# A scratch tile moved, dependences per 8 bytes, and new durations in the planner of a four-layer spectral kernel

## The chip, the cores and the metric

The kernel runs on one core of one Trainium2 chip. The metric is device time in microseconds (us), the median of several runs. The core has TensorE (PE; its weight loads are PEld), VectorE (DVE), ScalarE (ACT), GpSimd (POOL) and SyncE (SP, which here only issues DMAs). They run their own instruction streams and wait for each other by semaphores.

## The reference

x is 2048 rows of 448 bf16 values. Two kinds of layers alternate, each added to x:

```
x = x + A(layernorm(x));  x = x + B(layernorm(x))
x = x + A(layernorm(x));  x = x + B(layernorm(x))

A(x) = irfft2(rfft2(x) * (w_r + 1j * w_i))        # over rows and columns
B(x) = relu(x @ w1 + b1)**2 @ w2 + b2             # 448 -> 1792 -> 448
```

Both spectral layers (A) have the same weights, and so have both feed-forward layers (B).

## The kernel before

The 2048 rows lie as 16 tiles of 128 partitions (x_sb). A spectral layer is done by matmuls with constant matrices, in stages. Stage A (`stage_A`, matrices Fs or FA_sb) transforms inside a tile and leaves its result, by ScalarE, in the tile XA: each of the 16 tiles fills 8 of the 128 columns of every block of XA. Stage TD (TD_sb) transforms along d and reads all of XA; there are eight items p, taken in the order 1 to 7 and then 0, and ScalarE puts each result into U. Stage B (G_sb) transforms the long axis, from U into EF. Stage W multiplies by the weights: VectorE alone, in 12 tensor-tensor instructions of up to 904 elements a group, from EF over the scratch tile tmp into Z. Its groups are item 1 (on EF of item 1), items 2 and 3, 4 and 5, 6 and 7, and last item 0. In the first layer TensorE mirrors weights in between (J_sb), and w1_aux prepares w1 (ones). Stage Bi (H_sb) transforms back from Z into VT: eight matmuls for each item, in two PSUM tiles of four. Stage TI (TI_sb) is the inverse along d: ScalarE evicts it into TIo, which is an alias of the memory of XA. Stage AI (FI_sb) reads TIo and its result is added to x by VectorE (line 725). `ln_B` then prepares the layernorm of the feed-forward layer (a square on ScalarE, some short VectorE instructions, a root), and SP transposes the tile into yT by DMA.

In the feed-forward layer h_part (W1_sb, yT) fills hbuf and o_tile (W2_sb, hbuf) sums a tile of x. After an o_tile of the first feed-forward layer, `second_A` takes the layernorm for the next spectral layer: statistics, root, reciprocal, then two VectorE instructions that write y of the tile into yA, and stage A from there. yA holds eight tiles; it is an alias of the first half of tmp. U, EF, Z, hbuf and xb share one arena.

No instruction order is written by hand. Every instruction is first recorded (`_Sched.add`) with its engine, what it reads and writes, a cost and a latency. `_pages` cuts an access into pages, and a shared page makes a dependence: a read after a write, a write after a read or a write. Matmuls that share a PSUM tile form one unit. A unit's priority is the longest path behind it plus a bias set by hand for each stage and item. `schedule()` then takes, over all engines, the unit that can start first by the modelled times, with priority deciding between equals; a matmul unit is held back until all that the readers of its PSUM tile depend on, and that was recorded earlier, has been placed. The result is one fixed order for each engine. On the chip each instruction waits only for its recorded dependences, by semaphores, and behind those before it on its engine. The modelled times do not act on the chip themselves.

The lines that carry names in the trace: 455 is `mm`, 474 is `act`, 478 is `tt`, 482 is `cp`, 487 is `ts`. As these helpers record nearly every operation, groups are told apart by their tiles. What the memory aliases look like:

```python
        yA = tmp[:].rearrange("p a b c d -> p (a b c d)")[:, 0:8 * D].rearrange("p (t d) -> p t d", t=8)
        TIo = XA[:].rearrange("p a b c d -> p (a b c d)")[:, 0:NT * 2 * HD].rearrange("p (t g d) -> p t g d", t=NT, g=2)
        U = arena[:, 0:16 * 2 * LW].rearrange("p (c l) -> p c l", c=16)    # LW = 226, HD = 224, D = 448, NT = 16
```

Of the kernel before, what the change touches and what calls it, by code (L numbers as in the profile page):

```python
# [13 lines left out]
HD = 224  # L14
NT = 16
# [139 lines left out]
def _res(a):  # L155
    return a.ap() if isinstance(a, _PsAP) else a


def _pages(ap):

    if isinstance(ap, _PsAP):
        return [ap.tile]
    pat = list(ap.ap)
    row = pat[0][0]
    name = ap.tensor.name
    off = np.array([ap.offset % row if row else ap.offset])
    for step, cnt in pat[1:]:
        off = (off[:, None] + step * np.arange(cnt)[None, :]).reshape(-1)
    pg = np.unique(off * mybir.dt.size(ap.dtype) // 32)
    return [(name, int(i)) for i in pg]  # L170


class _Sched:
# [12 lines left out]
        self.reads_since = {}  # L186
        self.bias = 0.0

    def add(self, eng, fn, reads=(), writes=(), is_dma=False, cost=100.0, lat=150.0):
        op = _Op(eng, fn, is_dma, cost, lat)  # L190
        rk = [k for a in reads for k in _pages(a)]
        wk = [k for a in writes for k in _pages(a)]
        deps = {}
        for k in rk:
            w = self.last_write.get(k)
            if w is not None:
                deps[id(w)] = w
        for k in wk:
            w = self.last_write.get(k)
            if w is not None:  # L200
                deps[id(w)] = w
            for rd in self.reads_since.get(k, ()):
                deps[id(rd)] = rd
        for k in rk:
            self.reads_since.setdefault(k, []).append(op)
        for k in wk:
            self.last_write[k] = op
            self.reads_since[k] = []
        op.gdeps = [d for d in deps.values() if d is not op]
        op.deps = [d for d in deps.values() if d is not op and not (d.eng == "pe" and eng == "pe")]  # L210
        tile = writes[0].tile if eng == "pe" else None
        if tile is not None and tile.unit is not None:
            u = tile.unit
        else:
            u = _Unit(eng, tile)
            u.bias = self.bias
            u.seq = len(self.units)
            self.units.append(u)
            if tile is not None:
                tile.unit = u  # L220
        for a in reads:
            if isinstance(a, _PsAP):
                a.tile.readers.append(op)
        op.unit = u
        u.ops.append(op)
        return op

    def schedule(self):
# [25 lines left out]
        done = {}  # L254
# [10 lines left out]
        def ready_of(u):  # L265
            if u not in ready:
                r, off = 0.0, 0.0
                for op in u.ops:
                    for d in op.gdeps:
                        if d.unit is not u:  # L270
                            same = d.eng == u.eng and not d.is_dma
                            r = max(r, done[d] + d.lat - off)
                    off += op.cost
                ready[u] = r
            return ready[u]

        def pick_banks(n, now):
            best = None
            for b in range(0, NB, n):
                ok = [bank_user[i] is None or all(op in done for op in bank_user[i].readers) for i in range(b, b + n)]  # L280
                if all(ok):
                    f = max(bank_free[b:b + n])
                    key = (max(f, now), bank_free[b ^ 1] <= now and n == 1, f)
                    if best is None or key < best[0]:
                        best = (key, f, b)
            return best and best[1:]

        total = len(self.units)
        while total:
            choice = None  # L290
            for e in self.ENGINES:
                best = None
                avail = {}
                for u in cand[e]:
                    r = ready_of(u)
                    if u.tile is not None:
                        if u.tile.n not in avail:
                            avail[u.tile.n] = pick_banks(u.tile.n, free[e])
                        if avail[u.tile.n] is None:
                            continue  # L300
                        r = max(r, avail[u.tile.n][0])
                    start = max(r, free[e])
                    key = (start, -u.prio, u.seq)
                    if best is None or key < best[0]:
                        best = (key, u)
                if best is not None and (choice is None or best[0] < choice[0]):
                    choice = best
            assert choice is not None, "no unit can run"
            start, u = choice[0][0], choice[1]
            e = u.eng  # L310
            cand[e].remove(u)
            total -= 1
            if u.tile is not None:
                b = pick_banks(u.tile.n, start)[1]
# [8 lines left out]
            t = start  # L323
# [44 lines left out]
def _free(ap):  # L368
    n = 1
    for step, cnt in list(ap.ap)[1:]:  # L370
        n *= cnt
    return n


def bass_interleave_layers__spectral_gfnet__dense_activation_squared_relu__prompt_kernel(nc, A_x, A_w_r, A_w_i, B_x, B_w1, B_b1, B_w2, B_b2, out):
# [4 lines left out]
    sch = _Sched()  # L380

    with ExitStack() as es:
        onchip = set()

        def sb(name, shape, dt=BF16):
            t = es.enter_context(nc.sbuf_tensor(name, shape, dt))
            onchip.add(t.name)
            return t

        x_sb = sb("x_sb", [P, NT, 4 * P])  # L390
        XA = sb("XA", [P, 2, 2, 16, P])
# [6 lines left out]
        tmp = sb("tmp", [P, 8, 2, 2, LW])  # L398
        yA = tmp[:].rearrange("p a b c d -> p (a b c d)")[:, 0:8 * D].rearrange("p (t d) -> p t d", t=8)
        VT = sb("VT", [P, 2, 2, NT, 16, 8])  # L400
        xr = VT[:].rearrange("p a b t c j -> p (a b t c j)")[:, 0:NT * HD].rearrange("p (t d) -> p t d", t=NT)
        TIo = XA[:].rearrange("p a b c d -> p (a b c d)")[:, 0:NT * 2 * HD].rearrange("p (t g d) -> p t g d", t=NT, g=2)
        yT = sb("yT", [P, NT, 4, P])
        Wn = yT[:].rearrange("p a b c -> p (a b c)")[:, 0:2 * 16 * 225].rearrange("p (r k l) -> p r k l", r=2, k=16)
        Wt = sb("Wt", [P, 32, LW])
# [47 lines left out]

        def mm(o, lhsT, rhs, start, stop, skip=False):
            sch.add("pe", lambda e: e.matmul(_res(o), lhsT, rhs, start=start, stop=stop, skip_group_check=skip),  # L455
                    [lhsT, rhs], [o], cost=max(_free(rhs) / 2.4 + 6.0, 64.0), lat=200.0)

        def nfree(o, i):
            return _free(o) if not isinstance(o, _PsAP) else _free(i)

        def act(o, i, func=ACT.Copy, bias=None, scale=None):
            kw = {}
            rd = [i]
            c = (nfree(o, i) + 205.0) / 1.2
            if bias is not None:
                kw["bias"] = bias
                rd.append(bias)
                c += 60.0
            if scale is not None:
                kw["scale"] = scale  # L470
                if not isinstance(scale, float):
                    rd.append(scale)
                    c += 60.0
            sch.add("act", lambda e: e.activation(o, _res(i), func, **kw), rd, [o], cost=c)  # L474

        def tt(o, a, b, op, eng="dve"):
            rate = 0.96 if isinstance(a, _PsAP) or eng == "pool" else 1.92
            sch.add(eng, lambda e: e.tensor_tensor(o, _res(a), b, op), [a, b], [o], cost=_free(o) / rate + 65.0)  # L478

        def cp(o, i, eng="dve"):  # L480
            rate = 0.96 if isinstance(i, _PsAP) or eng == "pool" else 1.92
            sch.add(eng, lambda e: e.tensor_copy(o, _res(i)), [i], [o], cost=_free(o) / rate + 65.0)  # L482

        def ts(o, i, s1, s2, op0, op1=None, eng="dve"):
            rd = [i] + [s for s in (s1, s2) if s is not None and not isinstance(s, float)]
            kw = {} if op1 is None else {"op1": op1}
            sch.add(eng, lambda e: e.tensor_scalar(o, i, s1, s2, op0=op0, **kw), rd, [o],  # L487
                    cost=_free(o) * 0.83 + 265.0 if eng == "pool" else _free(o) / 1.92 + 65.0)

        def memset(o, v, eng="dve"):  # L490
            sch.add(eng, lambda e: e.memset(o, v), [], [o], cost=_free(o) / 1.92 + 60.0)

        def small(fn, reads, writes, cost=100.0):
            sch.add("dve", fn, reads, writes, cost=cost)


# [31 lines left out]
        def w1_aux():  # L528

            qs = []  # L530
            for i in range(4):
                f = slice(D * i, D * (i + 1))
                q = _Tile(1)
                qs.append((f, q))
                for blk in range(4):
                    mm(q[lambda b: ps[:, b, 0:D]], ones[:], W1_sb[:, blk, f], blk == 0, blk == 3)
                act(W1_sb[64:97, 3, f], q[lambda b: ps[64:97, b, 0:D]], ACT.Copy, scale=-1.0 / D)
                act(c_rem[64:97, f], q[lambda b: ps[64:97, b, 0:D]], ACT.Copy, scale=-1.0 / D)
            for r in (65, 67):
                dma("sp", W1_sb[r:r + 1, 3, :], B_b1.rearrange("(o f) -> o f", o=1))  # L540
            lo, c = W1_sb[96:97, 3, :], c_rem[96:97, :]
            tt(lo, c, lo, ALU.subtract)
# [369 lines left out]
```

## Time and profile before

| | |
|---|---|
| runs shown | 321.12 us median of 3 (320.16 to 321.24) |
| profiled execution | 323.18 us, of which the profile's span is 321.4 us |
| mean granted TensorE clock | 0.968 of 2.4 GHz |
| busy | PE 283.2 us (88%), DVE 195.9 (61%), ACT 184.4 (57%), POOL 17.1 (5%) |
| instructions | PE 1710 matmuls, DVE 606, ACT 381, POOL 34 |

Busy times are of the whole span. The kernel passes through a first spectral layer to about 70 us, a feed-forward layer to about 171 us, a second spectral layer to about 223 us and a second feed-forward layer. The busy share of an engine says little over all of them; the stage does. Matmuls overlap in their pipeline, so the distance of their starts is what TensorE needs for one, and the duration of a row of n like matmuls is n - 1 such distances and one whole duration. The same holds for evictions on ScalarE that follow each other.

### The profile page before, as it was taken

The page shows a single profiled execution, that of the slowest core. Times are in us where ns is not written, and L with a number is a line of the kernel's source. Part 1 is how long each engine was busy: PE and PEld are TensorE (multiplying, and loading weights), DVE is VectorE, ACT ScalarE, POOL GpSimd, SP SyncE. Part 2 cuts the span into 40 slices and gives each one's busy share as a digit, 9 for nine tenths or more (in the row PEclk, how much of TensorE's full clock was granted, in tenths as well). Part 3 has the DMA queues.
Part 4 walks back from the last instruction along what each step waited for, and adds up shares of the span by engine and source line. Part 5 has one row for each costly group of instructions (what it writes and reads, how often), then busy time and mean ns, then how long its engine had stood idle before and what let it go on. Part 6 is the DMA issues. An engine that isn't in the chain of part 4 may idle for free.

```text
span 321.4 us, 4833 instructions
## 1 busy us (share of the span) xinstructions
PE 283.2 (88%) x1710; PEld 168.5 (52%) x1710; DVE 195.9 (61%) x606; ACT 184.4 (57%) x381; POOL 17.1 (5%) x34
## 2 busy tenths in 40 slices
PE   0799895879999999999996966787999999999995
PEld 0466663748544544654454644464864454455442
DVE  5763998497684784576564489449733453474431
ACT  2479996899237437835713866479931741751720
POOL 3672000000000000000000000000000000000000
PEclk9989998999999999999999899599999999999999
DMA  7996000032100100030000000003701002005001
GB/s 231 423 382 175 1 2 1 0 77 56 35 1 0 24 10 1 2 65 2 0 0 2 0 0 2 2 0 65 101 14 46 0 22 70 0 14 107 4 14 43
DMA packets 25436, 16.04 MB, mean 50 GB/s; under 512 B 17666, under 2 KB 24322, under 8 KB 25412
## 3 DMA queue, kind: packets, MB, share of 16 engines
q1 hardware_dynamic: 25124, 15.44, 17.5%
q10 hardware_dynamic: 288, 0.30, 0.3%
q8 instruction: 13, 0.21, 0.3%
q14 instruction: 11, 0.09, 0.1%
HBM read 9.70 MB, written 1.84 MB: 36 GB/s over the span
## 4 chain that ended last, share of the span: by engine, by line
PE 73%; DVE 15%; ACT 6%; issue 3%; DMA 2%; POOL 1%; SPq 0%; DVEq 0%; ACTq 0%
PE ps L455 73%; DVE tmp L478 8%; DVE arena L478 3%; ACT arena L474 2%; ACT XA L474 2%; DVE x_sb L725 2%; DMA x_sb<-in_A_x_dram 1%; ACT VT L474 1%; DMA yT<-x_sb 1%; DVE st L567 1%; POOL Fs L487 1%; ACT sq_out L733 0%; DVE x_sb L773 0%; ACT W_sb L474 0%; DVE x_sb L482 0%
## 5 line engine op out<-in xcount | busy, mean ns | idle before, releaser
L474 ACT ACTIVATE arena<-ps 128x512 bf16<-128x512 f32 (+2 forms) x172 | 98.6, 590 | 56.9 <-PE ps L455 54.6
L455 PE MATMUL ps<-yT,W_sb 128*128 128x512 bf16 (+1 forms) x560 | 98.3, 336 | 2.0 <-ACT XA L474 1.3
L455 PE MATMUL ps<-W_sb,arena 128*128 128x448 bf16 x448 | 86.9, 352 | 0.0
L455 PEld LDWEIGHTS ps<-yT,W_sb 128*128 128x128 bf16 x560 | 54.7, 98 | 44.5 <-issue 2.8
L478 DVE TENSOR_TENSOR arena<-arena 128x512 bf16<-128x512 bf16 (+1 forms) x140 | 51.5, 372 | 40.1 <-ACT arena L474 34.9
L455 PEld LDWEIGHTS ps<-W_sb,arena 128*128 128x128 bf16 x448 | 43.8, 98 | 39.3
L474 ACT ACTIVATE XA<-ps 128x512 bf16<-128x512 f32 (+2 forms) x50 | 32.8, 679 | 20.2 <-PE ps L455 20.0
L773 DVE SCALAR_TENSOR_TENSOR x_sb<-ps,r,arena 128x448 bf16<-128x448 f32 x32 | 21.9, 684 | 31.3 <-PE ps L455 31.3
L455 PE MATMUL ps<-H_sb,arena 128*128 128x256 bf16 x128 | 22.2, 330 | 10.2 <-DVE arena L478 8.9
L725 DVE SCALAR_TENSOR_TENSOR x_sb<-ps,x_sb 128x448 bf16<-128x448 f32 x32 | 18.9, 620 | 16.4 <-PE ps L455 16.4
L474 ACT ACTIVATE VT<-ps 128x512 bf16<-128x512 f32 (+1 forms) x36 | 18.5, 552 | 10.9 <-PE ps L455 10.6
L455 PEld LDWEIGHTS ps<-H_sb,arena 128*128 128x128 bf16 x128 | 13.8, 116 | 18.4 <-DVE arena L478 12.8
L474 ACT ACTIVATE mv<-mv,epst 128x1 f32<-128x1 f32 (+1 forms) x24 | 7.1, 294 | 28.3 <-DVE mv L568 27.8
L567 DVE BATCH_NORM_STATS2 st<-x_sb 128x6 f32<-128x448 bf16 x32 | 19.4, 616 | 3.1 <-DMA x_sb<-in_A_x_dram 2.6
L733 ACT ACTIVATE sq_out<-x_sb 128x448 bf16<-128x448 bf16 x32 | 18.1, 568 | 3.0 <-DVE x_sb L725 2.8
L455 PE MATMUL ps<-Fs,x_sb 128*128 128x256 bf16 x32 | 10.2, 335 | 10.8 <-POOL Fs L487 8.9
L478 DVE TENSOR_TENSOR tmp<-arena 128x904 bf16<-128x904 bf16 (+1 forms) x16 | 8.9, 567 | 15.6 <-ACT arena L474 15.5
L455 PE MATMUL ps<-arena,G_sb 128*128 128x452 bf16 (+1 forms) x72 | 14.6, 335 | 3.9 <-ACT arena L474 3.9
L455 PE MATMUL ps<-XA,FI_sb 128*128 128x448 bf16 (+1 forms) x72 | 14.8, 332 | 3.2 <-ACT XA L474 2.3
L455 PE MATMUL ps<-TD_sb,XA 128*128 128x226 bf16 x128 | 16.0, 278 | 1.1 <-ACT XA L474 0.8
L478 DVE TENSOR_TENSOR tmp<-tmp,Wt 128x904 bf16<-128x904 bf16 (+1 forms) x32 | 16.4, 564 | 0.1
L455 PE MATMUL ps<-TI_sb,VT 128*128 128x224 bf16 x128 | 14.4, 259 | 1.5 <-ACT VT L474 1.5
(51 smaller groups left out, 202.9 us busy)
## 6 DMA issues: line engine op xcount, KB each, us to landing
out_dram<-x_sb SPq DMA_DIRECT2D x16, 112.0 KB, 1.7
W_sb<-in_B_w_dram SPq DMA_DIRECT2D x1, 1568.0 KB, 17.2
x_sb<-in_A_x_dram SPq DMA_DIRECT2D x3, 448.0 KB, 6.3
W_sb<-in_B_w_dram SPq DMA_DIRECT2D x1, 1344.0 KB, 15.5
yT<-in_A_w_r_dram SPq DMA_DIRECT2D x1, 900.0 KB, 8.9
yT<-in_A_w_i_dram SPq DMA_DIRECT2D x1, 900.0 KB, 10.4
H_sb<-c_H SPq DMA_DIRECT2D x1, 896.0 KB, 11.4
G_sb<-c_G SPq DMA_DIRECT2D x1, 672.0 KB, 8.1
```

The source lines that it names most:

```text
L455: sch.add("pe", lambda e: e.matmul(_res(o), lhsT, rhs, start=start, stop=stop, skip_group_check=skip), [lhsT, rhs], [o], cost=max(_free(rh ...
L474: sch.add("act", lambda e: e.activation(o, _res(i), func, **kw), rd, [o], cost=c)
L478: sch.add(eng, lambda e: e.tensor_tensor(o, _res(a), b, op), [a, b], [o], cost=_free(o) / rate + 65.0)
L487: sch.add(eng, lambda e: e.tensor_scalar(o, i, s1, s2, op0=op0, **kw), rd, [o], cost=_free(o) * 0.83 + 265.0 if eng == "pool" else _free(o ...
L567: small(lambda e, t=t: e.bn_stats(st[:, t, 0:6], x_sb[:, t, 0:D]), [x_sb[:, t, 0:D]], [st[:, t, 0:6]], 540.0)
L725: small(lambda e, xx=xx, r=r, i=i: e.scalar_tensor_tensor(out=xx, in0=_res(r), scalar=1.0, in1=xx, op0=ALU.mult, op1=ALU.add, accum_out=sd ...
L733: sch.add("act", lambda e, i=i: e.activation(sq_out[:, i % 2, :], x_sb[:, i, 0:D], ACT.Square, accum_out=sd[:, i, 1:2]), [x_sb[:, i, 0:D]] ...
L773: small(lambda e: e.scalar_tensor_tensor(out=o, in0=_res(i), scalar=r2[:, t, 0:1], in1=xb[:, t, :], op0=ALU.mult, op1=ALU.add), [i, r2[:, ...
```

## The change

The diff has three parts. TIo becomes an alias of tmp, the scratch of stage W, and no longer of XA. Pages are of 8 bytes in place of 32. And the costs and latencies that the planner is given change: a matmul costs N / 2.4 + 2.5 ns (at least 56) and not + 6 (at least 64); an ACT instruction from PSUM (N + 61) / 1.2, one from SBUF (N + 112) / 1.2, and not (N + 205) / 1.2 for both, with 93 ns and not 60 for a bias or a scale operand; VectorE instructions get 4 ns more; the short ones 75 ns and not 100; the default latency is 130 ns and not 150; and a matmul unit that depends on another unit may start 80 ns later.

```diff
@@ _pages
-    pg = np.unique(off * mybir.dt.size(ap.dtype) // 32)
+    pg = np.unique(off * mybir.dt.size(ap.dtype) // 8)
@@ _Sched.add
-    def add(self, eng, fn, reads=(), writes=(), is_dma=False, cost=100.0, lat=150.0):
+    def add(self, eng, fn, reads=(), writes=(), is_dma=False, cost=100.0, lat=130.0):
@@ _Sched.schedule, ready_of
-                            r = max(r, done[d] + d.lat - off)
+                            r = max(r, done[d] + d.lat + (80.0 if u.eng == "pe" else 0.0) - off)
@@ the kernel's tiles
-        TIo = XA[:].rearrange("p a b c d -> p (a b c d)")[:, 0:NT * 2 * HD].rearrange("p (t g d) -> p t g d", t=NT, g=2)
+        TIo = tmp[:].rearrange("p a b c d -> p (a b c d)")[:, 0:NT * 2 * HD].rearrange("p (t g d) -> p t g d", t=NT, g=2)
@@ mm
-                    [lhsT, rhs], [o], cost=max(_free(rhs) / 2.4 + 6.0, 64.0), lat=200.0)
+                    [lhsT, rhs], [o], cost=max(_free(rhs) / 2.4 + 2.5, 56.0), lat=195.0)
@@ act
-            c = (nfree(o, i) + 205.0) / 1.2
+            c = (nfree(o, i) + (61.0 if isinstance(i, _PsAP) else 112.0)) / 1.2
             if bias is not None:
-                c += 60.0
+                c += 93.0
             if scale is not None:
                 if not isinstance(scale, float):
-                    c += 60.0
+                    c += 93.0
@@ tt (cp alike)
-            sch.add(eng, lambda e: e.tensor_tensor(o, _res(a), b, op), [a, b], [o], cost=_free(o) / rate + 65.0)
+            sch.add(eng, lambda e: e.tensor_tensor(o, _res(a), b, op), [a, b], [o], cost=_free(o) / rate + 69.0)
@@ ts
-                    cost=_free(o) * 0.83 + 265.0 if eng == "pool" else _free(o) / 1.92 + 65.0)
+                    cost=_free(o) * 0.83 + 245.0 if eng == "pool" else _free(o) / 1.92 + 69.0)
@@ small
-        def small(fn, reads, writes, cost=100.0):
+        def small(fn, reads, writes, cost=75.0):
```

## Rows read from the trace of the kernel before

**Rows 1.** The page's chain that ended last: share of the span by engine.

```profile
PE 73%; DVE 15%; ACT 6%; issue 3%; DMA 2%; POOL 1%; SPq 0%; DVEq 0%; ACTq 0%
```

**Rows 2.** Busy time by stretch, us from the start; PEclk: granted clock.

```profile
core 0: us, PE busy (x) PEld busy (x) DVE busy (x) ACT busy (x) POOL busy (x), PEclk, DMA share, GB/s
...
48.00:52.50 4.50, 0.33 (x2) 0.10 (x1) 4.50 (x12) 2.79 (x7) 0.00 (x0) 1.00 0.00 2
52.50:58.20 5.70, 4.89 (x28) 3.32 (x28) 2.27 (x2) 4.30 (x9) 0.00 (x0) 0.70 0.00 0
58.20:69.67 11.47, 9.08 (x71) 6.49 (x72) 8.59 (x42) 10.11 (x25) 0.00 (x0) 1.00 0.14 29
...
133.00:171.30 38.30, 38.29 (x214) 20.91 (x215) 23.57 (x70) 18.07 (x39) 0.00 (x0) 1.00 0.07 15
...
204.10:211.50 7.40, 6.08 (x28) 3.60 (x28) 0.26 (x1) 4.35 (x9) 0.00 (x0) 0.59 0.01 2
```

**Rows 3.** TensorE in time, 24 to 60 us: start, duration, group, idle before.

```profile
32.95 0.60 PE L455 MATMUL ps<-H_sb,arena 128*128 128x256 bf16 x4
...
52.51 4.80 PE L455 MATMUL ps<-H_sb,arena 128*128 128x256 bf16 x27 [0.63 <-DVE arena L478]
...
58.25 1.61 PE L455 MATMUL ps<-TI_sb,VT 128*128 128x224 bf16 x15 [0.85 <-ACT VT L474]
```

**Rows 4.** VectorE in time, 24 to 60 us.

```profile
31.41 0.96 DVE L478 TENSOR_TENSOR arena<-tmp 128x226 bf16<-128x226 bf16 x4
32.74 1.29 DVE L478 TENSOR_TENSOR tmp<-arena 128x904 bf16<-128x904 bf16 x2 [0.37 <-ACT arena L474]
...
50.84 1.91 DVE L478 TENSOR_TENSOR arena<-tmp 128x452 bf16<-128x452 bf16 x6
```

**Rows 5.** TensorE in time, 174 to 226 us.

```profile
175.33 4.10 PE L455 MATMUL ps<-TD_sb,XA 128*128 128x226 bf16 x24 [0.78 <-ACT XA L474]
179.22 1.79 PE L455 MATMUL ps<-arena,G_sb 128*128 128x452 bf16 x8
...
184.48 0.72 PE L455 MATMUL ps<-H_sb,arena 128*128 128x256 bf16 x4
...
204.12 1.68 PE L455 MATMUL ps<-H_sb,arena 128*128 128x256 bf16 x7 [0.52 <-DVE arena L478]
206.48 4.13 PE L455 MATMUL ps<-H_sb,arena 128*128 128x256 bf16 x20 [0.69 <-ACT VT L474]
```

**Rows 6.** VectorE in time, 174 to 214 us.

```profile
183.68 0.97 DVE L478 TENSOR_TENSOR arena<-tmp 128x226 bf16<-128x226 bf16 x4
185.74 1.29 DVE L478 TENSOR_TENSOR tmp<-arena 128x904 bf16<-128x904 bf16 x2 [1.09 <-ACT arena L474]
...
202.46 1.91 DVE L478 TENSOR_TENSOR arena<-tmp 128x452 bf16<-128x452 bf16 x6
```

**Rows 7.** ScalarE in time, 174 to 187 us.

```profile
179.47 2.56 ACT L474 ACTIVATE arena<-ps 128x904 bf16<-128x904 f32 x3 [0.58 <-PE ps L455]
182.26 3.37 ACT L474 ACTIVATE arena<-ps 128x904 bf16<-128x904 f32 x4 [0.24 <-PE ps L455]
```

**Rows 8.** TensorE in time, 128 to 136 us.

```profile
130.72 0.93 PE L455 MATMUL ps<-XA,FI_sb 128*128 128x448 bf16 x4 [0.25 <-ACT XA L474]
131.48 1.04 PE L455 MATMUL ps<-FA_sb,tmp 128*128 128x256 bf16 x8
133.01 1.91 PE L455 MATMUL ps<-FA_sb,tmp 128*128 128x256 bf16 x16 [0.49 <-DVE sd L478]
```

**Rows 9.** ScalarE in time, 39 to 48 us.

```profile
40.08 2.07 ACT L474 ACTIVATE VT<-ps 128x512 bf16<-128x512 f32 x4
```

**Rows 10.** All engines in time, 0 to 25 us.

```profile
12.40 0.60 ACT L474 ACTIVATE XA<-ps 128x512 bf16<-128x512 f32 x1 [0.39 <-PE ps L455]
...
12.90 0.29 ACT L474 ACTIVATE mv<-mv,epst 128x2 f32<-128x2 f32 x1
...
14.13 0.27 PE L455 MATMUL ps<-Fs,x_sb 128*128 128x256 bf16 x1 [1.76 <-issue]
```

**Rows 11.** All engines in time, 24 to 72 us.

```profile
69.67 2.56 PE L455 MATMUL ps<-yT,W_sb 128*128 128x256 bf16 x22 [1.27 <-ACT XA L474]
```

More of the change, by code (lines that the diff above doesn't have):

```diff
@@ L477, in tt @@
             rate = 0.96 if isinstance(a, _PsAP) or eng == "pool" else 1.92
-            sch.add(eng, lambda e: e.tensor_tensor(o, _res(a), b, op), [a, b], [o], cost=_free(o) / rate + 65.0)
+            sch.add(eng, lambda e: e.tensor_tensor(o, _res(a), b, op), [a, b], [o], cost=_free(o) / rate + 69.0)
         def cp(o, i, eng="dve"):
             rate = 0.96 if isinstance(i, _PsAP) or eng == "pool" else 1.92
-            sch.add(eng, lambda e: e.tensor_copy(o, _res(i)), [i], [o], cost=_free(o) / rate + 65.0)
+            sch.add(eng, lambda e: e.tensor_copy(o, _res(i)), [i], [o], cost=_free(o) / rate + 69.0)
         def ts(o, i, s1, s2, op0, op1=None, eng="dve"):
```

## The prediction

> **What bounds the kernel now.** I began with the chain that ended last [rows 1]: TensorE carries 73% of it and VectorE 15%, so most of the span is matmuls in a row, and only what leaves TensorE idle can be won. The table of stretches [rows 2] says where that is. From 133 to 171.3 us TensorE is busy 38.29 of 38.30 us, and a planner cannot shorten that. In 48 to 52.5 us it is busy 0.33 of 4.50 us while VectorE is busy for all 4.50 us: that is the W product. Behind it, in 52.5 to 58.2 us, the granted clock is 0.70, a mixture of the two levels, 1.2 and 2.4 GHz; in the second layer's like stretch, 204.1 to 211.5 us, it is 0.59. So each spectral layer has a stage where VectorE sets the end, and a tail where TensorE works off what waited for VectorE, mostly at 1.2 GHz. Then comes a stage (58.2 to 69.67 us) where ScalarE is busy 10.11 of 11.47 us and TensorE only 9.08.
>
> I then read TensorE's and VectorE's order of time in both spectral layers [rows 3 to 6]. After W, 27 inverse matmuls (H_sb) start at 52.51 us and take 4.80 us, (4.80 - 0.28) / 26 = 0.174 us each [rows 3]. In the second layer 7 take 1.68 us and 20 take 4.13 us, about (4.13 - 0.27) / 19 = 0.203 us each [rows 5]. But the inverse work does not all wait for the last W: four H_sb matmuls run at 32.95 us, and four at 184.48 us, right after the first W group ended (31.41 + 0.96 = 32.37 us; 183.68 + 0.97 = 184.65 us) [rows 3 to 6]. Stage Bi(1) has eight matmuls in two tiles of four. Only one tile ran. Items 6, 7 and 0 make 24 matmuls, and at least 27 run at the end (27; 7 + 20): the other tile is among them.
>
> **Dependences per 8 bytes.** A row of U, EF or Z has 226 bf16, 452 bytes. Two neighbouring pairs of U meet at multiples of 1,808 bytes, which is 56.5 pages of 32 bytes but exactly 226 of 8. Two false dependences follow in the kernel before.
>
> First, the last Z row of item 0 shares a page with the first Z row of item 1. The columns 0 to 127 that Bi(1)'s first tile reads include that page; the second tile starts at column 97 and misses it. So the first tile waits for W(0), the last item. That is the half that ran late. Undone, four matmuls leave each tail and run in TensorE's idle time under W. At each tail's own rate this is 4 x 0.174 = 0.70 us in the first layer and, with (1.68 - 0.39) / 6 = 0.215 us from the seven right behind W, 4 x 0.215 = 0.86 us in the second; I take 1.55 us for both. The low end is nothing: the first tail ran partly at the higher level, and with less work under W its remaining 24 matmuls could all go at 0.215 us, 5.16 us instead of 4.80, a loss of 0.36 us there.
>
> Second, U pairs 2 and 3 (and 4 and 5, 6 and 7) share a page, so TD(3)'s eviction counts as overwriting what B(2) reads. The planner also holds a matmul unit back until what its reader depends on is placed, so TD(3) itself must follow B(2) in TensorE's order. The trace agrees: the first 24 TD matmuls hold only three of the eight items, then come B(1) and B(2) as eight matmuls at 179.22 us, and then a TD again. W(2,2) needs EF(3), hence TD(3) and B(3). VectorE, done with W(1,1) at 32.37 and 184.65 us, therefore idles 0.37 us and 1.09 us [rows 4, 6]. With TD(3) free to be third, B(3) can follow B(2) at about 179.22 + 1.79 = 181.0 us; ScalarE's three evictions from 179.47 us end at 182.03, and the next then ends about 182.03 + 0.82 = 182.9 us [rows 7], before 184.65. So I take both waits away whole, 0.37 + 1.09 = 1.46 us; the low end is nothing, if the new order puts another item there. What follows is dense on VectorE to its last Z write (50.84 + 1.91 = 52.75 us, 202.46 + 1.91 = 204.37 us), so an earlier start of W(2,2) becomes an earlier end.
>
> The other shared pages (XA and VT halves of 16 bytes) lie between instructions of ScalarE itself, which are in order anyway: nothing.
>
> **The inverse d-transform in tmp.** TIo's 16 x 448 elements fit in tmp. Its readers and writers from the W product are done at 52.75 us, and the first eviction into TIo comes with the TI matmuls at 58.25 us [rows 3]: 5.5 us cover the new dependence, which the data path through Z and VT imposes as well. Nothing is added. What goes away is that the second spectral layer's stage A writes XA across the whole tile, so it had to follow all reads of TIo. The trace shows just that: no FA_sb matmul before 131.48 us, directly behind the last AI at 130.72 us [rows 8]. In this clump TensorE waits 0.25 us for TIo's eviction and 0.49 us more at 133.01 us. With y of tile t only overlaying TIo rows of tiles below 8, stage A can be spread and other work fills these waits: 0.74 us. The low end is nothing, if the AI pair stays where it is with no free work beside it.
>
> **The planner's durations.** They move no instruction by themselves; they change the order. The new laws are close to rows: a 256-column matmul costs 109.2 ns by the new law, and 22 in 2.56 us with one of 0.27 us make 109.0 [rows 11, 10]; a 512-element eviction costs 573 / 1.2 = 478 ns instead of 598, and four take 2.07 us, so (2.07 - 0.60) / 3 = 490 ns [rows 9]; 904 elements cost 804 ns instead of 924, and (3.37 - 0.92) / 3 = 817 ns [rows 7]. What a reader waits is not shortened as much, as 130 + 80 ns follow where TensorE reads. VectorE's change is +4 ns.
>
> The better order could win the following and no more: TensorE's 1.76 us at 14.13 us, where ScalarE's root for the next tiles, at 12.90 us, stands behind an eviction at 12.40 us [rows 10]; 1.27 us at 69.67 us, where TensorE waits for a TIo eviction though the next layer's matmuls need none [rows 11]; and 1.38 us by which VectorE needs longer for the same W work in the first layer (32.74 to 52.75, 20.01 us) than in the second (185.74 to 204.37, 18.63 us) [rows 4, 6]. Together that is 4.41 us. It could also lose: orders of a list planner move when any cost moves, and I bound this by the largest wait of these, 1.76 us. I take nothing, between the two.
>
> The trace was weighed against one rule here. The Trainium skill, "ScalarE: Activation LUTs", section "What ACT_TABLE_LOAD costs", gives an ACTIVATE 186 ns + 0.833 ns per element, less about 93 ns when they stand back to back, whatever the source: an estimate of 520 ns for 512 elements and 846 for 904. By that the new planner charges 42 ns too little for each eviction from PSUM and would run ScalarE late; with the nine TIo evictions of each layer, in the stage where ScalarE is nearly full, 18 x 0.042 = 0.8 us would be lost, and the time would be 318.2. The rows above (490 and 817 ns) stand nearer to the new law, and I follow them.
>
> **The sum.** 1.55 + 1.46 + 0.74 = 3.75 us off the profiled execution's 323.18 us gives 319.4. That execution is 2.06 us above the median of the runs, 321.12, and the saved waits do not depend on that: 317.4 us.
>
> **The rivals.**
> 1. The order improves further, by 14.13 and 69.67 us both: 1.76 + 1.27 = 3.03 us more, 314.3. For it: the new laws fit the rows. Against: the wait at 14.13 us hangs on when x arrives, and those costs are unchanged. Chance 0.17.
> 2. The change does not do what it says: the false waits go, but VectorE's start and the tails stay, because TensorE's order is set by other priorities, or the lower clock takes back what the four matmuls leave (0.36 us lost in the first tail against 0.86 won in the second). Between 320.6 and 321.1, say 320.7. Against: both waits coincide with the shared pages. Chance 0.19.
> 3. Slower: stage A, now free to come early, makes TensorE wait for y. From the end of an output tile to y stand eight steps on VectorE and ScalarE, behind other tiles' work. Twelve tiles (all but the last four) each waiting as at 133.01 us cost 12 x 0.49 = 5.9 us: 321.12 - 3.75 + 5.9 = 323.3. It decides from (3.75 + 1.6) / 12 = 0.45 us a tile. Against: from 133 to 171.3 us TensorE is busy 38.29 of 38.30 us with stage A of most tiles inside [rows 2]. With a new order for other reasons that loses as much, chance 0.13.
>
> My forecast has the remaining 0.51.
>
> **How the numbers follow.** About 0.5% (1.6 us) is what a measurement of this kernel can tell from no change. Forecast and rival 1 lie below 319.5: with a little of the forecast's mass lost to its low ends, 0.67. Rival 2 is the same, 0.19, with an upper edge of it slower; rival 3 with that, 0.14. The range goes from 317.4 - 4.4 = 313.0, less a little, to 322.0, which holds rival 2 and part of the losing orders and leaves out some 0.1 above and 0.1 below. The forecast's own range is 315.5 to 319.5.
>
> **What would show it.** Right: in the changed profile an FA_sb matmul stands well before the last AI; eight H_sb matmuls run together after the first W group, and 24, not 28, after the last; VectorE has no wait between W(1,1) and W(2,2). Wrong: VectorE's W work still ends as long after the first TD matmul as before, or TensorE shows many waits for VectorE's y between 85 and 171 us. The prediction falls if the stages before the feed-forward (TI and AI; 11.47 us in the first layer) get slower by a new order, which I have not priced tile by tile.

## The result, and the profile after

The changed kernel takes 311.17 us (median of 4 runs, 310.72 to 312.5), the kernel before beside it on the same chip 321.18 us: ratio 0.9696, 95% interval 0.9654 to 0.9738. That is 10.0 us where 3.75 were forecast, and below the range. The profiled execution of after takes 312.5 us with a span of 310.7 us. Medians below are of runs in the faster of the two states that the chip shows; one run of T alone and one of P with D were in the slower one and are left out.

The page's chain that ended last, of after, answers to [rows 1]:

```profile
PE 72%; ACT 11%; DVE 10%; issue 3%; DMA 1%; POOL 1%; SPq 0%; DVEq 0%; POOLq 0%
```

VectorE's part fell from 15% to 10%. To see where, I cut both spans at the same events and read their starts off the orders of time: the first TD matmul of a layer, VectorE's start on item 1, the start of its second group (items 2 and 3), its last Z write, the 23 or more inverse matmuls behind W, and the first long row of TI. After minus before, in us:

| stretch | first layer | second layer |
|---|---|---|
| first TD to VectorE's first W instruction | +0.52 | -0.09 |
| first W group, item 1 | -0.20 | -0.22 |
| wait ahead of the second W group | -0.37 | -1.09 |
| second W group to the last Z write | -1.07 | -0.06 |
| tail of inverse matmuls starts ahead of the last Z write, by 2.13 and no longer 0.24 | -1.89 | -1.88 |
| start of that tail to the long row of TI matmuls | -1.27 | -3.31 |
| sum | -4.28 | -6.65 |

The rest, from the profiled executions too: stage A of the first layer +0.65, from the first TI row to the last output tile of the first feed-forward layer -1.17, from there to TD -0.09, from the second TI row to the last output tile +0.88. In all -10.66 us (318.15 to 307.49 us for the start of the last output tile's sum). So nearly all of it lies in the two W stages and the tails behind them. Both executions ran the second layer's TD at the lower clock (24 matmuls in 4.10 and 3.98 us), so that is not in the difference.

VectorE in time in after, first layer, then second:

```profile
32.59 0.84 DVE L478 TENSOR_TENSOR arena<-tmp 128x226 bf16<-128x226 bf16 x4
33.34 1.16 DVE L478 TENSOR_TENSOR tmp<-arena 128x904 bf16<-128x904 bf16 x2
...
49.09 1.30 DVE L478 TENSOR_TENSOR arena<-tmp 128x452 bf16<-128x452 bf16 x4
50.31 1.17 DVE L478 TENSOR_TENSOR tmp<-arena,Wt 128x904 bf16<-128x904 bf16 x2
51.39 0.89 DVE L478 TENSOR_TENSOR arena<-tmp 128x452 bf16<-128x452 bf16 x2
...
178.70 0.84 DVE L478 TENSOR_TENSOR arena<-tmp 128x226 bf16<-128x226 bf16 x4
179.45 1.16 DVE L478 TENSOR_TENSOR tmp<-arena 128x904 bf16<-128x904 bf16 x2
```

The same stretch of before, four lines that [rows 4] leave out:

```profile
48.69 0.62 DVE L478 TENSOR_TENSOR tmp<-tmp 128x904 bf16<-128x904 bf16 x1
49.23 0.62 DVE L478 TENSOR_TENSOR tmp<-arena,Wt 128x904 bf16<-128x904 bf16 x1
49.77 0.62 DVE L478 TENSOR_TENSOR tmp<-tmp 128x904 bf16<-128x904 bf16 x1
50.30 0.62 DVE L478 TENSOR_TENSOR tmp<-arena,Wt 128x904 bf16<-128x904 bf16 x1
```

Three things are to be seen. The waits ahead of the second group are gone (33.34 us follows 32.59 + 0.84). The pair that took 1.29 us [rows 4, 6] takes 1.16, so its two starts are 0.54 us apart and no longer 0.67. And W(0), the instructions that read Wt at 49.23 and 50.30 us of before, stood between those of items 6 and 7, and its Z writes were in the last clump of six. After, items 6 and 7 write their Z at 49.09 us in one piece, and W(0) comes behind it.

TensorE in time in after:

```profile
33.58 1.03 PE L455 MATMUL ps<-H_sb,arena 128*128 128x256 bf16 x8 [0.51 <-ACT arena L474]
...
36.70 2.52 PE L455 MATMUL ps<-TD_sb,XA 128*128 128x226 bf16 x24
...
50.15 3.13 PE L455 MATMUL ps<-H_sb,arena 128*128 128x256 bf16 x23 [0.17 <-DVE arena L478]
...
54.62 1.60 PE L455 MATMUL ps<-TI_sb,VT 128*128 128x224 bf16 x15 [0.34 <-ACT VT L474]
...
87.06 1.04 PE L455 MATMUL ps<-FA_sb,tmp 128*128 128x256 bf16 x8
...
132.22 0.92 PE L455 MATMUL ps<-tmp,FI_sb 128*128 128x448 bf16 x4
...
179.87 1.03 PE L455 MATMUL ps<-H_sb,arena 128*128 128x256 bf16 x8
...
195.28 0.28 PE L455 MATMUL ps<-H_sb,arena 128*128 128x256 bf16 x1 [1.61 <-DVE arena L478]
195.89 3.12 PE L455 MATMUL ps<-H_sb,arena 128*128 128x256 bf16 x23 [0.33 <-DVE arena L478]
199.97 1.60 PE L455 MATMUL ps<-TI_sb,VT 128*128 128x224 bf16 x15 [0.30 <-ACT VT L474]
```

All that the prediction named as signs is there: eight H_sb behind the first W group, 24 (1 and 23) in the tail, no wait of VectorE ahead of the second W group, FA_sb matmuls at 87.06 us, 45 us ahead of the last AI. But the tail is also a different one. Its 23 matmuls take 0.13 us each, not 0.174 and 0.203 to 0.215. The table of stretches of after says why:

```profile
50.10:54.60 4.50, 3.35 (x24) 2.19 (x25) 2.83 (x6) 4.36 (x11) 0.00 (x0) 1.00 0.01 2
...
128.00:134.00 6.00, 6.00 (x38) 3.49 (x36) 4.14 (x14) 3.35 (x8) 0.00 (x0) 1.00 0.00 0
195.80:200.00 4.20, 3.32 (x25) 2.17 (x26) 2.11 (x6) 3.20 (x8) 0.00 (x0) 1.00 0.02 4
```

The granted clock in the tails is 1.00, where it was 0.70 and 0.59 [rows 2].

### The profile page after: what moved, and what is told of

Same layout as the page of the kernel before. It is cut to its first block, busy times and chain, and to the rows that moved or that the text cites. A ratio compares the mean times of both kernels' runs of the same rounds, so it can differ in the third digit from the quotient of the medians.

```text
span 310.7 us, 4816 instructions
## 1 busy us (share of the span) xinstructions
PE 279.3 (90%) x1710; PEld 166.4 (54%) x1710; DVE 192.7 (62%) x606; ACT 181.8 (58%) x381; POOL 17.3 (6%) x34
## 4 chain that ended last, share of the span: by engine, by line
PE 72%; ACT 11%; DVE 10%; issue 3%; DMA 1%; POOL 1%; SPq 0%; DVEq 0%; POOLq 0%
PE ps L455 72%; DVE tmp L478 5%; ACT arena L474 4%; ACT VT L474 3%; DVE x_sb L725 2%; DVE arena L478 2%; ACT sq_out L733 1%; DMA x_sb<-in_A_x_dram 1%; ACT XA L474 1%; ACT Wt L474 1%; DVE st L567 1%; POOL Fs L487 1%; DVE x_sb L773 0%; ACT sd L474 0%; ACT tmp L474 0%
## 5 line engine op out<-in xcount | busy, mean ns | idle before, releaser
L455 PE MATMUL ps<-yT,W_sb 128*128 128x512 bf16 (+1 forms) x560 | 99.7, 337 | 2.8 <-ACT arena L474 2.5
L474 ACT ACTIVATE XA<-ps 128x512 bf16<-128x512 f32 x32 | 18.4, 596 | 19.2 <-PE ps L455 19.2
L455 PE MATMUL ps<-H_sb,arena 128*128 128x256 bf16 x128 | 17.0, 273 | 3.9 <-DVE arena L478 2.4
L455 PE MATMUL ps<-Fs,x_sb 128*128 128x256 bf16 x32 | 11.2, 361 | 10.2 <-POOL Fs L487 10.2
L474 ACT ACTIVATE VT<-ps 128x512 bf16<-128x512 f32 (+1 forms) x36 | 17.2, 599 | 2.3 <-PE ps L455 2.3
L455 PE MATMUL ps<-arena,G_sb 128*128 128x452 bf16 (+1 forms) x72 | 13.9, 333 | 3.6 <-ACT VT L474 3.0
L455 PEld LDWEIGHTS ps<-H_sb,arena 128*128 128x128 bf16 x128 | 11.8, 98 | 8.6 <-DVE arena L478 6.3
L474 ACT ACTIVATE tmp<-ps 128x896 bf16<-128x896 f32 (+1 forms) x18 | 14.7, 827 | 2.9 <-PE ps L455 2.9
L455 PE MATMUL ps<-tmp,FI_sb 128*128 128x448 bf16 (+1 forms) x72 | 14.7, 332 | 1.6 <-ACT tmp L474 1.5
```

## The experiments

Every ratio is to the kernel before on the same chip, with its 95% interval. The first six are the parts of the change, alone and in pairs; their edits are the diff's own lines, so only the names of the parts are given: P for the line in `_pages`, T for TIo in tmp, D for all costs and latencies.

**P alone.**

```diff
-    pg = np.unique(off * mybir.dt.size(ap.dtype) // 32)
+    pg = np.unique(off * mybir.dt.size(ap.dtype) // 8)
```

> The kernel before with pages of 8 bytes and nothing else. Theory V (the false dependences inside VectorE's W product, between neighbouring rows of tmp and of Z, were the large part: the planner spread the W groups over each other and the chip waited between them): nearly the whole gain is here, 312 to 315 us; VectorE's 904-element instructions stand 0.54 us apart, the W groups follow each other without mixing, and W of item 0 is last. Theory L (the new durations order the work better): at most the 3.75 us of the prediction's first terms, 317.5 us or more.

**D alone.** All lines of the diff but those of `_pages` and TIo.

> The kernel before with the new costs and latencies and nothing else. Theory L: most of the gain, 311 to 316 us. Theory V: no gain, 319 to 323 us, with the W groups mixed on VectorE as before and the same waits of about 0.1 us between neighbouring rows.

**T alone.**

```diff
-        TIo = XA[:].rearrange("p a b c d -> p (a b c d)")...
+        TIo = tmp[:].rearrange("p a b c d -> p (a b c d)")...
```

> The kernel before with TIo in tmp and nothing else. Both theories: the two waits of 0.25 and 0.49 us behind the last AI go, stage A is spread over the feed-forward layer, 320.0 to 321.2 us. If the prediction's third term is wrong, 321.2 us or more.

**P and T.**

> Pages of 8 bytes and TIo in tmp, with the costs of before. Theory V: what the full change reaches within 2 us, 310 to 313 us. Theory L: no better than 317 us.

**P and D.**

> Pages of 8 bytes and the new durations; TIo stays over XA. Theory B (pages and durations only work together: the pages let the W groups follow each other without mixing, and the new durations keep the last pair's stage B ahead of Bi): 311 to 314 us, no wait over 1 us of VectorE for EF between W groups. Theory T (moving TIo is needed for it too, since pages alone cost 4 us and pages with TIo 2 us): 318 us or more.

**D and T.**

> The new durations and TIo in tmp; pages of 32 bytes. Theory B: no better than the two parts alone, 318 to 322 us, W groups mixed on VectorE and 0.65 us between T0 and T1. Theory T: 314 us or less.

| parts | us | ratio | interval |
|---|---|---|---|
| P | 325.87 | 1.0125 | 1.0071 to 1.0180 |
| D | 321.15 | 0.9971 | 0.9940 to 1.0003 |
| T | 320.49 | 0.9967 | 0.9929 to 1.0004 |
| P, T | 323.66 | 1.0044 | 1.0009 to 1.0079 |
| P, D | 317.68 | 0.9899 | 0.9863 to 0.9935 |
| D, T | 316.02 | 0.9850 | 0.9826 to 0.9874 |
| P, D, T | 311.17 | 0.9696 | 0.9654 to 0.9738 |

No part carries the gain. The 8-byte pages alone cost 1.25%, and every theory that gave one part most of the gain falls with this table. The effects do not add: the three parts alone sum to a gain by D and T and a loss by P, +0.6% in all, and together they give -3.0%. The durations are worth 0.3% by themselves (an interval that reaches no change), 1.2% on top of T (0.9967 to 0.9850) and 3.5% where P and T are in (1.0044 to 0.9696). D with T lies between the ranges of both theories. By the same events as above it needs 110.89 us in the first feed-forward stretch (113.03 before) and 32.10 us from TD to TI in the second layer (36.18 before, of which 1.5 us is the lower clock in TD), so half of the gain comes without P.

What P alone does to the W stage is in its trace. VectorE, then TensorE in time:

```profile
47.78 1.17 DVE L478 TENSOR_TENSOR tmp<-arena 128x904 bf16<-128x904 bf16 x2 [4.34 <-ACT arena L474]
...
54.82 2.02 DVE L478 TENSOR_TENSOR W_sb<-c_rem,W_sb 1x1792 bf16<-1x1792 f32 x1
56.87 0.39 DVE L478 TENSOR_TENSOR arena<-tmp 128x452 bf16<-128x452 bf16 x1
```

```profile
43.19 2.00 PE L455 MATMUL ps<-H_sb,arena 128*128 128x256 bf16 x15 [0.33 <-DVE arena L478]
45.03 0.92 PE L455 MATMUL ps<-W_sb,ones 128*128 128x448 bf16 x4
45.79 0.93 PE L455 MATMUL ps<-arena,G_sb 128*128 128x452 bf16 x4
46.56 0.95 PE L455 MATMUL ps<-TD_sb,XA 128*128 128x226 bf16 x8
```

VectorE's groups are dense, the false waits are gone, and then it waits 4.34 us for EF. TensorE's order has turned: the last TD, at 46.56 us, stands behind inverse matmuls and w1 work, where after does its last TD at 36.70 us. The freedom that the smaller pages gave was used to put work of low urgency first. An instruction for w1 (54.82 us) got ahead of W(0)'s last Z write besides. But this is not where P alone loses. From the first TD matmul to the long row of TI its two spectral layers take 34.52 and 33.75 us, together 1.5 us less than before (33.58 and 36.18), since less is left behind W. The loss stands behind them: from the TI row to the last output tile 116.59 us and not 113.03 in the first feed-forward layer, 108.63 and not 106.64 in the second, with one wait of 2.08 us, at 69.82 us, for a TIo that is still over XA. P with T needs only 112.43 and 105.35 us there; it loses by waits for EF, which the second layer has too, 2.50 and 5.35 us, so that this layer takes 39.66 us. Without P, in D, T and both, W(0) stays mixed into items 6 and 7 and the pair stays at 1.29 us.

P with D has the W stage of after in the first layer, but TIo is still over XA. The stretches of its trace around the last AI:

```profile
126.00:132.40 6.40, 3.58 (x31) 2.59 (x29) 3.64 (x16) 6.39 (x18) 0.00 (x0) 1.00 0.01 3
132.40:142.30 9.90, 9.82 (x44) 4.78 (x45) 4.78 (x16) 0.80 (x4) 0.00 (x0) 0.83 0.28 53
```

From 125.69 to 130.1 us TensorE runs 32 FA_sb matmuls in one clump; then ScalarE is busy 6.39 of 6.40 us, TensorE is idle for 2.8 us and then has a granted clock of 0.83. In after, 128 to 134 us are full. From the first hidden matmul to the last output tile this kernel needs 105.87 us, after 101.08. So T, priced at 0.74 us, is worth 4.8 us of this stretch with P and D in. From the TI row to the last output tile it is worth 4.2 us with P in (116.59 to 112.43) and 0.9 us alone (113.03 to 112.09), near its price: it is the small pages that make TIo over XA dear, and why was not traced further. A second, lower-clocked tail (0.66 from 200 to 205 us) is in P with D too. The profiled execution, 318.81 us, is one of the slower of this kernel, whose runs go from 315.91 to 319.35 us.

**P, T and only the new ScalarE law of D.**

```diff
-            c = (nfree(o, i) + 205.0) / 1.2
+            c = (nfree(o, i) + (61.0 if isinstance(i, _PsAP) else 112.0)) / 1.2
...
-                c += 60.0
+                c += 93.0
```

> Pages of 8 bytes, TIo in tmp, and of the durations only the new law of a ScalarE instruction. Theory A (of the durations it is the cost of an eviction that matters: charged 120 ns too much, ScalarE looks like the bound of stage W, and the planner lets Bi's evictions go ahead of the last pair's): all of the gain in both W stages, 310 to 314 us. Theory M (the other laws are needed: matmul, latencies, 80 ns): VectorE waits over 2 us for the last pair's EF again, 318 to 324 us.

310.47 us, ratio 0.9687 (0.9647 to 0.9728): all of the gain. TensorE's order of TD, B and Bi in the W stages is that of after. Of the durations, this one law is enough.

**After with only this law put back.**

```diff
-            c = (nfree(o, i) + (61.0 if isinstance(i, _PsAP) else 112.0)) / 1.2
+            c = (nfree(o, i) + 205.0) / 1.2
...
-                c += 93.0
+                c += 60.0
```

> The changed kernel with the one law of before for ScalarE's costs, (N + 205) / 1.2 and 60 ns for a bias; all else of the new durations stays. Theory A (the new ScalarE law alone carries the share of the durations; with the old one the planner takes ScalarE for the bound of stage W and puts inverse matmuls and VT evictions ahead of the last pairs' forward ones): the first layer's W stage, from its first instruction to its last Z write, takes 27 to 29 us and not 22.1, with a wait of 4 us for EF on VectorE; 313.5 to 317.5 in all, ratio 0.977 to 0.989. Rival M (the durations matter together, and each alone restores most): 310 to 312, ratio 0.966 to 0.972.

315.73 us, 0.9774 (0.9699 to 0.9850). VectorE in time in this kernel:

```profile
47.29 1.17 DVE L478 TENSOR_TENSOR tmp<-arena 128x904 bf16<-128x904 bf16 x2 [5.03 <-ACT arena L474]
```

The first layer's W stage takes 28.86 us (after 22.14), as expected of theory A; the second is after's, 21.77 us to 21.76, where P with T alone needs 29.78. So the other durations mend the second layer, and the ScalarE law mends both. The other durations without it take P with T from 1.0044 to 0.9774, most of the way, and that interval just overlaps after's; so the law is enough, but theory A's claim that it alone carries the share of the durations does not hold. Why the law does it is argued, not shown: by the old one an eviction of 904 elements is 924 ns, by the new 804, with 817 in the trace [rows 7], so that the old planner has ScalarE behind by 0.12 us for each eviction of U, EF and VT and sees no hurry in the forward matmuls.

**The order of before, with the chip's waits by 8-byte pages.** The planner still sees 32-byte pages; only the semaphore waits are by 8 bytes.

```diff
+        op.gdeps = self._find(op, reads, writes, 32, self.last_write, self.reads_since)
+        fine = self._find(op, reads, writes, 8, self.last_write8, self.reads_since8)
+        op.deps = [d for d in fine if not (d.eng == "pe" and eng == "pe")]
```

> The kernel before in its own order, planned with pages of 32 bytes; only the waits that are put out go by pages of 8 bytes. Theory W (the chip's own waits between neighbouring rows on VectorE, about 0.1 us each, are a part by themselves): the first layer's W stage 1.0 to 1.5 us shorter and the second's 0.3 us, 319.3 to 320.3 us. Theory O (only the order counts): as before, 321 us or more.

320.02 us, 0.9949 (0.9920 to 0.9979). VectorE in time (the lines of the helpers are six further down in this kernel):

```profile
31.65 1.17 DVE L484 TENSOR_TENSOR tmp<-arena 128x904 bf16<-128x904 bf16 x2 [0.49 <-ACT arena L480]
...
48.25 0.62 DVE L484 TENSOR_TENSOR tmp<-arena,Wt 128x904 bf16<-128x904 bf16 x1
48.79 1.91 DVE L484 TENSOR_TENSOR arena<-tmp 128x452 bf16<-128x452 bf16 x6
```

The pair is at 1.17 us with the order untouched: the 0.13 us more of before was VectorE waiting on a semaphore of its own. From the second group to the last Z write it is 19.05 us instead of 20.01, in the second layer 18.38 instead of 18.63. The false waits of all engines together are worth 0.5%; the rest of the gain needs another order.

**W(0) first.** After, with W(0) at highest priority.

```diff
+                sch.bias += 1e6        # ahead of the four instructions of W(0)
+                sch.bias -= 1e6        # behind them
```

> The changed kernel, with the four VectorE instructions of W(0) at highest priority: in the first layer W(0) goes ahead of the last three scratch instructions of W(6,2), in the second behind its first Z writes; TensorE's order in the W stages is unchanged. Theory T (the gain comes from where W(0) stands: in the changed kernel the inverse matmuls of items 6 and 7 start before W(0) ends, under its 1.9 us): these matmuls start 1.3 to 1.9 us later in each layer, and the end comes 2.0 to 3.8 us later, ratio to before 0.976 to 0.982. Rival D (only the dense VectorE order matters and W(0) is hidden behind ScalarE's evictions of VT): within 0.8 us of the changed kernel, ratio 0.968 to 0.972.

312.50 us, 0.9688 (0.9634 to 0.9741): by the ratio the time of after, by the medians 1.3 us above it. Theory T's times lie above the interval, so as a statement on the whole gain it falls; an effect of 1 to 2 us is not excluded by an interval of 1.7 us to either side. The trace of this kernel says more; TensorE in the second layer, then its stretch:

```profile
194.65 0.28 PE L455 MATMUL ps<-H_sb,arena 128*128 128x256 bf16 x1 [2.99 <-DVE arena L478]
195.26 4.10 PE L455 MATMUL ps<-H_sb,arena 128*128 128x256 bf16 x23 [0.33 <-DVE arena L478]
...
200.05 1.61 PE L455 MATMUL ps<-TI_sb,VT 128*128 128x224 bf16 x15 [0.49 <-ACT VT L474]
```

```profile
194.00:200.00 6.00, 4.59 (x25) 3.02 (x25) 1.81 (x6) 3.49 (x8) 0.00 (x0) 0.72 0.01 3
```

TD starts there at 168.32 us (170.44 in after), so the tail comes 26.94 us behind TD instead of 25.45, with a clock of 0.72, and the long TI row 31.73 us instead of 29.53: 2.2 us. In the first layer that row comes 29.37 us behind TD, in after 29.30: nothing. Evictions of the w1 work and of VT keep ScalarE going there, which may be the reason. So W(0)'s place matters in the second layer alone. From its TD to the last output tile 1.7 us of the 2.2 are left (138.75 us to 137.05); that the profiled execution ends no later than after's is due to its first stage A, 23.14 us and not 25.32; in the traces of all kernels this stage ends between 22.96 and 25.32 us.

**Work for TensorE under W.** The kernel before with 26 added matmuls in each spectral layer, whose results nobody reads.

```diff
+                if p0 == 6:
+                    for k in range(2, 8):
+                        fill(T[k][:, 0], 3)
...
+                if p0 == 6:
+                    for k in range(4):
+                        fill(z[:, :, k], 2)
```

> The kernel before, with 26 added matmuls in each spectral layer (128x128 weights, 224 to 904 columns of VectorE's own operands) that read what VectorE has just finished in the group of items 6 and 7 and whose results nobody reads; the planner places them at lowest priority. It tests the clock by itself. Theory C (part of the gain is the clock: before, the tail of inverse matmuls behind W runs at a granted clock of 0.70 and 0.59 because TensorE stood still under W; in the changed kernel it runs at 1.00): if work under W keeps the clock up, the first tail, 4.80 us, shrinks by up to 1.3 us and the second, 5.81 us, by up to 2 us, less what the added matmuls take in front of them; 318.5 to 320, ratio 0.992 to 0.997. Theory N (the lower clock in the tail costs nothing, since evictions of VT on ScalarE end last there): time of before plus up to 1 us, ratio 1.000 to 1.003, with the granted clock risen all the same.

320.72 us, 0.9970 (0.9938 to 1.0002). TensorE in time and the stretches of this kernel, first layer:

```profile
52.31 3.40 PE L455 MATMUL ps<-H_sb,arena 128*128 128x256 bf16 x28 [1.01 <-DVE arena L478]
55.55 1.69 PE L455 MATMUL ps<-arena,FI_sb 128*128 128x452 bf16 x8
```

```profile
48.00:52.50 4.50, 3.49 (x20) 1.64 (x18) 4.50 (x12) 2.62 (x6) 0.00 (x0) 1.00 0.01 2
52.50:58.20 5.70, 5.69 (x48) 4.40 (x47) 2.08 (x2) 4.26 (x11) 0.00 (x0) 1.00 0.00 0
```

With TensorE at work under W the tail is granted 1.00, and 28 matmuls take 3.40 us where 27 took 4.80 [rows 3]. The time is at the edge of theory C's range, with an interval that reaches no change. Eight of the added matmuls (1.69 us) stand between the tail and TI, so of its 1.4 us about 1.0 is left: the row of TI comes 4.52 us behind the last Z write and not 5.50, in the second layer 5.25 and not 7.14. Behind that it is lost again: from the second TI row to the last output tile this kernel takes 110.01 us and not 106.64, with eleven of the layer's 26 added matmuls there. The clock is shown; its worth in this place is not.

**Work for TensorE ahead of TD.** P, T and the ScalarE law, with 12 added matmuls whose results nobody reads where TensorE waits for the last tile's layernorm.

```diff
+            if t == NT - 1:
+                fill(x_sb[:, t, 0:D], 8)
...
+            if t == NT - 1:
+                fill(y[:, 0:D], 4)
```

> 8-byte pages, TIo in tmp and the new ScalarE law alone, with 12 added matmuls whose results nobody reads, placed where TensorE waits for the last tile's layernorm ahead of the second layer's TD. Theory C (a stretch in which TensorE stands still is followed by matmuls at the lower clock: the 24 matmuls of TD there take 3.98 us in the changed kernel, about 2.5 us at full clock): 1.0 to 1.5 us faster than the same kernel without them, ratio to before 0.963 to 0.966. Theory N (the stage is paced by ScalarE's evictions of U, 24 x 0.82 us, whatever TensorE's clock): no change, ratio 0.967 to 0.970.

308.71 us, 0.9582 (0.9530 to 0.9633), the fastest of all. TensorE in time with the added matmuls, then without them:

```profile
166.11 1.69 PE L455 MATMUL ps<-x_sb,FI_sb 128*128 128x448 bf16 x8 [0.34 <-DVE x_sb L773]
...
168.47 0.92 PE L455 MATMUL ps<-tmp,FI_sb 128*128 128x448 bf16 x4
169.33 2.53 PE L455 MATMUL ps<-TD_sb,XA 128*128 128x226 bf16 x24
```

```profile
168.04 0.75 PE L455 MATMUL ps<-FA_sb,tmp 128*128 128x256 bf16 x4 [2.12 <-DVE tmp L487]
169.56 4.15 PE L455 MATMUL ps<-TD_sb,XA 128*128 128x226 bf16 x24 [0.78 <-ACT XA L474]
```

The 24 TD matmuls take 2.53 us and not 4.15, and VectorE's first W instruction comes 4.40 us behind TD and not 5.96. All later stretches agree within 0.05 us, so the 1.6 us stay to the end. That is a little more than theory C expected, and theory N falls.

## Why the prediction was wrong, point by point

**The terms of the sum.** The two false waits (1.46 us) are gone whole, as forecast. The four matmuls have left each tail (1.55). 128 to 134 us, where 0.74 us of waits stood, is busy 6.00 of 6.00 us. So each mechanism was right, and so were the signs that should show it. None of the rivals happened as told: TensorE does not wait for y, but for the last tile's (2.12 us, before 1.68), the lower clock took nothing back, and of the two waits of rival 1 the first is still there (1.78 us, where 1.76 stood at 14.13 us), and in place of the second stands one of 0.90 us for an eviction into hbuf.

**What failed first** is the step on the pages, "The other shared pages ... lie between instructions of ScalarE itself, which are in order anyway: nothing." It looked at XA and VT only. Neighbouring rows of tmp, 1,808 bytes apart, and of Z, 452 bytes, share pages too, and their writer is VectorE, the engine that sets the end of the stage. In before it waited there on itself (1.29 us a pair, 1.16 without), which together with the other engines' false waits is 0.5% by the run that undid these alone; and the planner had mixed W(0) into items 6 and 7. That the mixing comes from the shared pages is seen from P alone, whose groups are dense. Being in order on an engine does not make a dependence on that engine free.

**What failed most** is "They move no instruction by themselves; they change the order ... I take nothing, between the two." With P and T in, the durations are worth 323.66 to 311.17 us, 11.2 us by the ratios (1.0044 - 0.9696, of 321); the bound of 4.41 us was read off waits of before, but most of what D prevents are waits that the kernel before did not have: P with T takes 39.66 us from TD to TI in the second layer, after 29.53, before 36.18. P's term, +3.01 us, measured by itself, is a loss of 1.25%, by the stretches behind TI. Adding terms was wrong for parts that meet in one planner. Rival 1 had the order improving too, at the wrong places.

**The tails** were priced "At each tail's own rate", the lower clock's. In after they are at 1.00, and from their start to TI 1.27 and 3.31 us are saved, 4.58 where 1.55 were expected. How this splits is worked out, not measured: four matmuls fewer at the old rates are those 1.55, the rest is the higher rate and the evictions that follow it. The kernel with added matmuls under W ties the rate to what TensorE did before; the gap right ahead does not settle it. Idle 1.61 and 0.33 us ahead of after's second tail gave 1.00, idle 2.99 and 0.33 gave 0.72, but idle 1.04 and 0.21 ahead of 15 such matmuls gave 0.59 in the kernel with the old ScalarE law (from 200.15 us).

**TIo in tmp** was mis-sized in company. Alone it is 0.3%, with an interval that reaches no change; on top of P and D 2.0% (0.9899 to 0.9696), 4.8 us of them in the feed-forward stretch.

**The rule weighed.** By the Trainium skill, "ScalarE: Activation LUTs", section "What ACT_TABLE_LOAD costs", whose figures do not say in which memory the operand lay, the new law charges evictions too little and would lose 0.8 us, an estimate. After's four evictions of 904 elements from 183.14 us take 3.37 us, as in [rows 7], 0.817 us each, and this law alone turns P with T from 323.66 into 310.47 us: row and time speak for the law.

Open is how much of W(0)'s place is in the final time (the interval is too wide), why small pages make TIo over XA dear, and why the old law makes the planner choose as it does, which was only argued.

## What to carry to other kernels

Where a planner writes the order, price its parts together: a freed dependence can lose by itself, because the old costs spend the freedom badly, and win once the costs fit. Look for false dependences between instructions of the limiting engine itself, not only across engines. And where a trace shows the lower clock behind a short gap, try to keep TensorE at work through it: twelve matmuls that nobody reads gave 1.6 us here.

## What the runs showed of the hardware that was not expected

- Two 904-element VectorE instructions start 0.54 us apart when neither waits, and 0.67 us (1.29 - 0.62) when the second waits for a semaphore of the first, on the same engine. Four Z writes take 1.30 us and not 1.56. The Trainium skill, "VectorE: DVE Perf Modes", section "The DRAIN you can't avoid", reports that a semaphore after each of eight instructions "costs nothing extra"; these rows do not agree, and the run that undid the false waits of all engines was 0.5% faster.
- With 2.12 and 0.78 us idle around four matmuls ahead of it, TD ran 24 matmuls in 4.15 us; with 0.34 us idle, in 2.53. The granted clock of those stretches, in this order, is 0.57 and 1.00:

```profile
169.50:173.50 4.00, 3.94 (x24) 3.29 (x25) 0.00 (x0) 1.85 (x2) 0.00 (x0) 0.57 0.01 4
```

```profile
170.00:174.00 4.00, 4.00 (x31) 2.85 (x30) 0.27 (x1) 3.68 (x5) 0.00 (x0) 1.00 0.02 4
```

- The same gaps do not always give the same clock. The kernel before, then the kernel with work under W:

```profile
173.80 0.75 PE L455 MATMUL ps<-FA_sb,tmp 128*128 128x256 bf16 x4 [1.68 <-DVE tmp L487]
175.33 4.10 PE L455 MATMUL ps<-TD_sb,XA 128*128 128x226 bf16 x24 [0.78 <-ACT XA L474]
```

```profile
172.19 0.75 PE L455 MATMUL ps<-FA_sb,tmp 128*128 128x256 bf16 x4 [1.69 <-DVE tmp L487]
173.72 2.52 PE L455 MATMUL ps<-TD_sb,XA 128*128 128x226 bf16 x24 [0.78 <-ACT XA L474]
```

  The granted clock of these two rows of TD is 0.59 and 1.00. With T, D, and D with T it is 1.00 behind the same gaps, and with 8-byte waits alone 0.60. So a single trace of such a place can mislead by 1.6 us.
